# Second MLP, second stage: seven block products in place of eight, weights kept split in DRAM, first-stage sums gathered in PSUM

## The chip, the cores and the metric

One core of a Trainium2 chip runs the whole program. The time is device microseconds from launch to end, as the median of several executions; lower is better. TensorE is called PE, VectorE DVE, ScalarE ACT, GpSimd POOL and SyncE SP. SP issues every DMA of this program.

## The reference

Attention over chunks (4 batches, 8 heads, 768 positions, head size 64; each chunk of 32 positions sees itself, 16 positions before, 8 after and 8 memory positions) gives 3072 tokens of 512 values. Two MLPs follow, each with 512 x 2048 and 2048 x 512 weights:

```python
def _moe_ref(x, w_in, w_out):
    h = x @ w_in
    g = h * (1.0 / (1.0 + np.exp(-h)))
    return (g @ w_out).astype(np.float32)

def _moe2_ref(x, w_in, w_out):
    h = x @ w_in
    r = np.maximum(h, 0.0)
    g = r * r
    return (g @ w_out).astype(np.float32)
```

q, k, v and the memory keys and values are float32, the MLP weights float64 (the kernel reads them as 64-bit words); the output is float32.

## The kernel before

**Precision.** PE multiplies in a float32 form of reduced precision. So every operand is split in two: a high part (a rounding copy, mostly on ACT) and a low part (operand minus high part, on DVE or POOL), and each matrix product is three matmuls, high x low, low x high and high x high, added up in one PSUM bank. "A split" below is this pair of operations.

**Staging.** After attention for the first block, the first MLP works through six blocks of 512 tokens (`mlp`, line 688). A block has 16 steps, one for each 128 of the 2048 inner values: 12 matmuls into a `ph` bank, Silu and split, and, some two steps later, 12 matmuls into four `acc` banks. Attention of the next block lies between. The result goes to DRAM (`y1`), transposed. In the same time `convert_out` (line 589) turns the second MLP's output weights from 64-bit words to float32 and stores them to DRAM (`w2s`). In the last block `convert_forms` (line 610) prepares seven combinations of the input weights, split, which stay in SBUF.

**The second MLP.** It works through six blocks of 512 tokens, and each block through eight pairs: a pair is two of the sixteen 128-wide parts of d_ff, k and k + 8. Its first product (x times w_in) is done by the Strassen-Winograd scheme: the 2 x 2 blocked product of a pair takes seven block products in place of eight. `tokens` (line 794) makes the seven combinations of x and splits them; `stage_in` (line 860) does the products P1 to P7 in the order of `PRODUCTS`, each six matmuls of 256 columns into its own bank (four banks `ph`, `ph`, `sc`, `sc` in turn), and DVE adds them up to the four quarters of h (`plus`). Then h is squared after max(h, 0), split, and `stage_out` (line 960) multiplies it with w_out the plain way: for each of the pair's two parts four tiles of three matmuls of 512 columns, into four `acc` banks that gather over the whole block. `stage_in` also loads the two parts of w_out (256 KB each) and splits them, once in each block. `second` (line 982) lists the turns: products of pair k, then the second stage of pair k - 1. `evict` (line 745) copies the four `acc` banks out at a block's end and stores them.

**What sets the order.** Every operation is a piece with a cost on each engine that may do it, a due time, and the pieces that it needs. `Graph.order` (line 107) places the pieces by simulated time, in order of due time, and the program is issued in that order, so that each engine's queue and SP's queue of DMAs are fixed before the run. `on_tensor` (line 788) keeps the second MLP's products on PE in the order in which they are written. Operations that use the port that DVE and POOL share carry `port=True`, and the planner doesn't overlap them. Buffers are named by tag, with a count for each (`pool`), and a piece that takes a buffer waits for the last users of the one it replaces.

Of the kernel before, what the change touches and what calls it, by code (L numbers as in the profile page):

```python
# [59 lines left out]
PRODUCTS = (1, 6, 5, 7, 2, 3, 4)  # L60
# [123 lines left out]
def chunk_attention_two_mlps(ctx, tc, units, weights, out):  # L184
# [23 lines left out]
    w2s = dram.tile([FT, P, DM], F32, name="w2s")  # L208
# [45 lines left out]
    IN, OUT = 4.95, 5.56  # L254
    PAIR = IN + OUT
    BLOCK2 = PAIRS * PAIR
# [329 lines left out]
    def out_due(i):  # L586
        return step_due(1, 8) + i * 3.5 * BLOCK1 / FT

    def convert_out(i):

        due = out_due(i)
        wraw, got = load_words(i, 1, due)
        got.release = due - 25
        wu, d = words(1, i, 1, due, wraw, 0, got)

        def store(e):
            nc.sync.dma_start(out=w2s[i], in_=wu.tile)

        w2_kept[i] = G.add({"SP": 0.45}, due + 2, store, [d], uses=[wu], size=P * DM * 4)
# [88 lines left out]
    def mlp(j):  # L688
        accs, earlier = None, []
        size = step_due(j, 1) - step_due(j, 0)  # L690
        for i in range(FT):
# [34 lines left out]
            def back(e, i=i, wb=wb, g=g):  # L726
                w, t = wb.tile, g.tile
                first, last = i == 0, i == FT - 1
                for m, acc in enumerate(accs):
# [4 lines left out]
                    nc.tensor.matmul(o, w[:, 0, ws], t[:, 0], start=False, stop=last)  # L734

            y = G.add({"PE": 2.8}, due + 2.4 * size, back, [d, w_done[i, 1]],
# [4 lines left out]
        ends = evict(accs, [y], due, lambda m: y1[m, :, j * TB:(j + 1) * TB])  # L741
        stored[j] = ends
        return y

    def evict(accs, y, due, where, last=False):
        ends = []
        for m, acc in enumerate(accs):
            yb = G.buf("xq" if last and m == KT - 1 else "wr")

            if last and m == KT - 1:  # L750

                for n in range(2):
                    def part(e, n=n, acc=acc, yb=yb):
                        t = yb.tile if n else take(yb, [P, DM], F32, "y")
                        cs = slice(n * HALF2, (n + 1) * HALF2)
                        (nc.vector.tensor_copy if n else nc.scalar.copy)(t[:, cs], acc.tile[:, cs])  # L756

                    def store(e, n=n, m=m, yb=yb):
                        cs = slice(n * HALF2, (n + 1) * HALF2)
                        nc.sync.dma_start(out=where(m)[:, cs], in_=yb.tile[:, cs])  # L760

                    a = G.add({"DVE" if n else "ACT": 0.4}, due, part,
                              [y[m % len(y)]] + [yb.by] * n, new=[yb] * (not n),
                              uses=[acc] + [yb] * n)
                    G.add({"SP": 0.45}, due, store, [a], uses=[yb], size=P * HALF2 * 4)
                continue
# [27 lines left out]
    def tokens(b, due):  # L794
# [35 lines left out]
        xs, four = {}, []  # L830
        for rank, n in enumerate(X_FORM[p] for p in PRODUCTS):

# [17 lines left out]
            a = G.add({"ACT": 0.62}, due - 6 + 0.8 * rank, high,  # L850
                      [ready[n]] + ([] if new else [x.by]),
                      new=[x] * new, uses=[xf] + [x] * (not new))
            xs[n] = (x, at, G.add({"DVE": 0.72, "POOL": 1.35}, due - 5 + 0.8 * rank, low, [a],
# [3 lines left out]
    in_bank = itertools.cycle(("ph", "ph", "sc", "sc"))  # L857
    w_place = itertools.cycle((f"w{FT - 2}", f"w{FT - 1}"))

    def stage_in(k, xs, due):  # L860

        where, converted = forms[k]
        bank = {n: G.buf(next(in_bank)) for n in PRODUCTS}
        left, right = (0, HALF2), (HALF2, T2)
        one, two = G.buf("pr"), G.buf("pts")
        s1, u2, u4, u3 = (one, left), (one, right), (two, left), (two, right)
        h = [G.buf("xq") for _ in range(2)]
        made = {}

        def product(n):  # L870
            x, xa, x_done = xs[X_FORM[n]]
            fb, fa = where[W_FORM[n]]

            def emit(e):
                o = take(bank[n], [P, HALF2], F32, "pp")
                w, t = fb.tile[:, fa], x.tile[:, xa]
                for kt in range(2):
                    ws = slice(kt * P, (kt + 1) * P)
                    for at, (a, c) in enumerate(((1, 0), (0, 1), (0, 0))):
                        nc.tensor.matmul(  # L880
                            o, w[:, a, ws], t[:, c, kt],
                            start=(kt == 0 and at == 0), stop=(kt == 1 and at == 2),
                        )

            made[n] = on_tensor(0.71, due, emit, [x_done, *converted], [bank[n]], [fb, x])

        def plus(at, to, n, other, after):

            (tb, (t0, t1)), (ob, (o0, o1)) = to, other
            new = not tb.users  # L890

            def emit(e):
                if new:
                    take(tb, [P, T2], F32, "sums")
                nc.vector.tensor_tensor(  # L895
                    tb.tile[:, t0:t1], bank[n].tile, ob.tile[:, o0:o1], op=ALU.add
                )

            return G.add({"DVE": 0.45}, due + at, emit, [made[n], *after], new=[tb] * new,
                         uses=[bank[n]] + [ob] * (ob is not tb) + [tb] * (not new))  # L900

        def copy_p1(e):
            nc.scalar.copy(take(one, [P, T2], F32, "sums")[:, :HALF2], bank[1].tile)

        for n in PRODUCTS:
            product(n)
        a1 = G.add({"ACT": 0.4}, due + 1, copy_p1, [made[1]], new=[one], uses=[bank[1]])
        a2 = plus(1.2, u2, 6, s1, [a1])
        a4 = plus(1.4, u4, 5, u2, [a2])
        a3 = plus(1.6, u3, 7, u2, [a2, a4])  # L910
        c22 = plus(1.8, (h[1], right), 7, u4, [a4])
        c11 = plus(2.5, (h[0], left), 2, s1, [a1])
        c12 = plus(3.0, (h[0], right), 3, u4, [a4, c11])
        c21 = plus(3.5, (h[1], left), 4, u3, [a3, c22])
        done = []
        for n, after in enumerate(([c12], [c21])):
            g = G.buf("g")

            def square(e, n=n):
                t = h[n].tile  # L920
                nc.vector.scalar_tensor_tensor(t, t, 0.0, t, op0=ALU.max, op1=ALU.mult)  # L921

            def high(e, n=n, g=g):
                t = take(g, [P, 2, T2], F32R, "g2")
                nc.scalar.copy(t[:, 0], h[n].tile)  # L925

            def low(e, n=n, g=g):
                t = g.tile
                engine[e].tensor_tensor(t[:, 1], h[n].tile, f(t[:, 0]), op=ALU.subtract)  # L929

            d = G.add({"DVE": 0.75}, due + 4 + n, square, after, uses=[h[n]], port=True)
            d = G.add({"ACT": 0.62}, due + 5 + n, high, [d], new=[g], uses=[h[n]])
            done.append((g, G.add({"DVE": 0.75, "POOL": 1.35}, due + 6 + n, low, [d],
                                  uses=[h[n], g], port=True)))
        w2 = G.buf(next(w_place))
        split = []
        for n in range(2):
            wf = G.buf("wu")

            def load(e, n=n, wf=wf):  # L940
                nc.sync.dma_start(out=take(wf, [P, DM], F32, "wf"), in_=w2s[k + n * PAIRS])

            def high(e, n=n, wf=wf):
                if n == 0:
                    take(w2, [P, 2, 2, DM], F32R, "w2")
                nc.scalar.copy(w2.tile[:, n, 0], wf.tile)  # L946

            def low(e, n=n, wf=wf):
                t = w2.tile[:, n]
                engine[e].tensor_tensor(t[:, 1], wf.tile, f(t[:, 0]), op=ALU.subtract)  # L950

            d = G.add({"SP": 0.45}, due - 8 + n, load, [w2_kept[k + n * PAIRS]], new=[wf],
                      size=P * DM * 4)
            d = G.add({"ACT": 0.62}, due + 4 + n, high, [d, *([w2.by] if n else [])],
                      new=[w2] * (n == 0), uses=[wf] + [w2] * n)
            split.append(G.add({"DVE": 0.75, "POOL": 1.35}, due + 5 + n, low, [d],
                               uses=[wf, w2], port=True))
        return done, w2, split

    def stage_out(k, n, made, accs, due, final):  # L960
        done, w2, split = made
        g, ready = done[n]
        first, last = k == 0 and n == 0, k == PAIRS - 1 and n == 1
# [131 lines left out]
```

## Time and profile before

| | us |
|---|---|
| median of 3 runs | 1134.35 |
| lowest and highest | 1133.68, 1135.42 |
| profiled execution, span from first to last instruction | 1133.1 |

The profile is of one execution; no time other than its span is given for it. Busy time of an engine is the time that its instructions cover; matmuls overlap, so that the distance between the starts of two matmuls, and not the duration shown, is what one costs. The granted clock is that of PE as a share of 2.4 GHz. A wait is put down to what ended it.

### The profile page before, as it was taken

What the parts mean: (1) busy time and instruction counts of PE and PEld (TensorE: products, weight loads), DVE (VectorE), ACT (ScalarE), POOL (GpSimd) and SP (SyncE); (2) the same over time, 40 slices, a digit from 0 to 9 for tenths busy, and PEclk for the clock granted to TensorE, in tenths of its full rate; (3) what the DMA queues carried; (4) which work ended last, traced back from release to release, by engine and by line L of the source; (5) the groups of instructions that cost most, each with busy time, mean ns of one, the idle gap of its engine ahead of it and who ended that gap; (6) DMA issues with size and microseconds to landing.
All of it is one profiled execution on the core that took longest, in us unless ns stands there. A gap on an engine that the chain in (4) does not pass through costs nothing. (4 is left out here: it accounts for less than half of the span.)

```text
span 1133.1 us, 21204 instructions
## 1 busy us (share of the span) xinstructions
PE 1114.5 (98%) x8620; PEld 932.4 (82%) x8620; DVE 756.3 (67%) x1717; ACT 463.1 (41%) x781; POOL 120.9 (11%) x105
## 2 busy tenths in 40 slices
PE   6999999999999999999999999999999999999998
PEld 4777777777777777778888888988988988988987
DVE  4777668776677777665688656656656656656654
ACT  2788743443334444343576223323323323323321
POOL 0032200000000000000001211211211211211110
PEclk8899999999999999999999999999999999999999
DMA  7765334232234223222335213313313313211311
GB/s 276 262 215 187 104 113 141 75 122 75 94 112 149 78 76 122 76 90 75 105 118 161 64 38 93 94 38 93 94 38 94 93 38 94 93 38 57 93 38 37
DMA packets 52849, 114.81 MB, mean 101 GB/s; under 512 B 5520, under 2 KB 11920, under 8 KB 52752
## 3 DMA queue, kind: packets, MB, share of 16 engines
q1 hardware_dynamic: 52752, 113.46, 31.0%
q8 instruction: 67, 1.10, 0.4%
q14 instruction: 30, 0.25, 0.1%
HBM read 96.67 MB, written 16.78 MB: 100 GB/s over the span
## 5 line engine op out<-in xcount | busy, mean ns | idle before, releaser
L880 PEld LDWEIGHTS pp<-xs,forms 128*128 128x128 f32 x2016 | 247.2, 188 | 4.6 <-DVE sums L895 0.5
L880 PE MATMUL pp<-xs,forms 128*128 128x256 f32 x2016 | 248.6, 282 | 0.2 <-DVE sums L895 0.2
L895 DVE TENSOR_TENSOR sums<-pp,sums 128x256 f32<-128x256 f32 x336 | 135.9, 423 | 70.1 <-PE pp L880 66.2
L699 PE MATMUL ph<-x,w 128*128 128x512 f32 x384 | 156.3, 407 | 2.7 <-DVE w L568 2.0
L925 ACT CAST g<-sums 128x512 fp32r<-128x512 f32 x96 | 59.5, 620 | 230.1 <-DVE sums L921 188.0
L700 PE MATMUL ph<-x,w 128*128 128x512 f32 x384 | 153.5, 400 | 0.0
L701 PE MATMUL ph<-x,w 128*128 128x512 f32 x384 | 153.2, 399 | 0.0
L971 PE MATMUL acc<-w,g 128*128 128x512 f32 x384 | 152.4, 397 | 0.7 <-POOL g L929 0.7
L732 PE MATMUL acc<-g,w 128*128 128x512 f32 x384 | 152.5, 397 | 0.1
L733 PE MATMUL acc<-g,w 128*128 128x512 f32 x384 | 152.3, 397 | 0.0
L972 PE MATMUL acc<-w,g 128*128 128x512 f32 x384 | 151.9, 396 | 0.0
L734 PE MATMUL acc<-g,w 128*128 128x512 f32 x384 | 151.7, 395 | 0.0
L970 PE MATMUL acc<-w,g 128*128 128x512 f32 x384 | 151.7, 395 | 0.0
L707 ACT ACTIVATE ph<-ph 128x512 f32<-128x512 f32 x96 | 55.9, 582 | 223.6 <-PE ph L701 223.5
L950 POOL TENSOR_TENSOR w<-wf,w 128x512 fp32r<-128x512 f32 x47 | 60.9, 1295 | 411.6 <-ACT w L946 411.6
L714 DVE TENSOR_TENSOR g<-ph,g 128x512 fp32r<-128x512 f32 x96 | 66.1, 689 | 48.1 <-ACT g L711 46.8
L946 ACT CAST w<-wf 128x512 fp32r<-128x512 f32 x96 | 59.1, 622 | 92.7 <-PE acc L972 89.6
L387 DVE STREAM_TRANSPOSE turned<-pr 32x128 f32<-32x128 f32 x256 | 77.5, 303 | 25.4 <-ACT pr L398 20.7
L929 DVE TENSOR_TENSOR g<-sums,g 128x512 fp32r<-128x512 f32 x95 | 65.9, 697 | 39.4 <-ACT g L925 36.5
L699 PEld LDWEIGHTS ph<-x,w 128*128 128x128 f32 x384 | 72.7, 189 | 23.1 <-DVE w L568 2.8
L732 PEld LDWEIGHTS acc<-g,w 128*128 128x128 f32 x384 | 72.1, 188 | 18.6 <-DVE w L568 0.2
L701 PEld LDWEIGHTS ph<-x,w 128*128 128x128 f32 x384 | 72.9, 190 | 17.3
(73 smaller groups left out, 1356.9 us busy)
## 6 DMA issues: line engine op xcount, KB each, us to landing
wf<-w2s SPq DMA_DIRECT2D x96, 256.0 KB, 2.7
wraw<-weights SPq DMA_DIRECT2D x40, 512.0 KB, 4.4
raw<-units SPq DMA_DIRECT2D x48, 384.0 KB, 4.4
raw<-units SPq DMA_DIRECT2D x48, 260.0 KB, 4.9
w<-weights SPq DMA_DIRECT2D x24, 512.0 KB, 6.1
y<-y SPq DMA_DIRECT2D x24, 256.0 KB, 2.4
xf<-y SPq DMA_DIRECT2D x24, 256.0 KB, 4.0
out<-y SPq DMA_DIRECT2D x23, 256.0 KB, 2.1
```

The costliest lines, as they stand in the source:

```text
L387: nc.vector.transpose(out=t[rs, :, cs], in_=src.tile[cs, :, rs])
L699: nc.tensor.matmul(o, w[:, 1, ws], x[:, 0, kt], start=(kt == 0), stop=False)
L700: nc.tensor.matmul(o, w[:, 0, ws], x[:, 1, kt], start=False, stop=False)
L701: nc.tensor.matmul(o, w[:, 0, ws], x[:, 0, kt], start=False, stop=(kt == KT - 1))
L732: nc.tensor.matmul(o, w[:, 1, ws], t[:, 0], start=first, stop=False)
L733: nc.tensor.matmul(o, w[:, 0, ws], t[:, 1], start=False, stop=False)
L734: nc.tensor.matmul(o, w[:, 0, ws], t[:, 0], start=False, stop=last)
L880: nc.tensor.matmul(o, w[:, a, ws], t[:, c, kt], start=(kt == 0 and at == 0), stop=(kt == 1 and at == 2),)
L895: nc.vector.tensor_tensor(tb.tile[:, t0:t1], bank[n].tile, ob.tile[:, o0:o1], op=ALU.add)
L970: nc.tensor.matmul(o, t[:, 0, gs], w[:, 1], start=first, stop=False)
L971: nc.tensor.matmul(o, t[:, 1, gs], w[:, 0], start=False, stop=False)
L972: nc.tensor.matmul(o, t[:, 0, gs], w[:, 0], start=False, stop=last)
```

## The change

The second stage of the second MLP becomes a seven-product scheme too, in the Winograd form, over the pair's two parts of d_ff (inner), the two halves of the 512 tokens and the two halves of the 512 outputs. Each of the seven products is six matmuls of 256 columns. They gather over the eight pairs of a block in six banks or seven, and only at the block's end are they combined (`combine`, `finish`) into the four quarters of the output: one copy and six adds, and one more add for the product P4.

- **Weights.** `convert_out` now works on pairs: it forms the combinations of w_out that the scheme needs (four differences), splits all seven forms, and stores the split parts to DRAM: `w2s` is (pairs, 7 forms, 128, 2, 256). In the second MLP they are loaded as they are and no longer split there. Per pair, `load_pair` loads forms in DMAs of 512 KB (two forms) and 256 KB (one).
- **Second stage's left operand.** Per pair, four quarters of h squared, A11, A12, A21 and A22, and the sums S1 to S4 of them, are made on DVE and POOL (`sums`) and split two at a time (`split`). A22 is kept until the next block, where the fourth product uses it.
- **First stage.** Its products are no longer kept apart and added by DVE: P1, P6, P7 and P4 are matmuls into the same half bank one after the other, and ACT copies the running sum out between them (`visit`, `kept_sum`); P2 and P5 go to the halves of a second bank, P3 is added to P5's half. Three adds per pair stay on DVE.
- **Order.** One step has the pair n's seven first-stage products, three second-stage products of pair n - 1 and three of n - 2 in between; the fourth products of a block (eight) are done in the second and third pair of the next block, those of the last block at the end, into the two `sc` banks.
- **First MLP's end.** The last 12 matmuls of its last block are cut into four parts that lie between the first products of the second MLP.
- **Buffers.** `wr` has four instead of three.

The diff, cut to its core:

```diff
-PRODUCTS = (1, 6, 5, 7, 2, 3, 4)
+PRODUCTS = (1, 2, 5, 6, 7, 4, 3)
+BACK = (1, 5, 6, 7, 3, 2)
+NF = len(BACK) + 1
+BANK = {1: "acc", 5: "ph", 6: "acc", 7: "acc", 2: "acc", 3: "ph"}
...
-        ("wu", 4), ("wr", 3), ("nm", 3), ("sm", 4),
+        ("wu", 4), ("wr", 4), ("nm", 3), ("sm", 4),
...
-    w2s = dram.tile([FT, P, DM], F32, name="w2s")
+    w2s = dram.tile([PAIRS, NF, P, 2, HALF2], F32, name="w2s")
...
+        t1 = diff((0, 0), b(ua, 1), b(ua, 0), [da], True)
+        t2 = diff((0, 1), b(ub, 1), t(0, 0), [t1, db], False)
+        t3 = diff((1, 0), b(ub, 1), b(ua, 1), [da, db], True)
+        t4 = diff((1, 1), b(ub, 0), t(0, 1), [t2, t3], False)
...
+        split([0], ua, lambda: halves(ua.tile)[:, :1], [da], 2)
+        split([5, 4], ub, lambda: halves(ub.tile), [db], 3)
+        split([1, 2], z[0], lambda: z[0].tile, [t2], 4)
+        split([3, 6], z[1], lambda: z[1].tile, [t4], 5)
...
+    def front(q, x, due):
+        at = q.k % 2
+        q.kept = pairs[q.n - 1].kept if at else G.buf(next(saved))
+        a1 = visit(q, 0, ((1, 0),), x, due[0])
+        u1 = kept_sum(q, U1, 0, 0, [a1], due[0] + 0.9, new=True)
+        yield
+        b1 = visit(q, 1, ((2, 1), (5, 0)), x, due[1])
+        c11 = plus(q, (q.t, A11), 1, 1, U1, [u1, b1], due[1] + 5)
+        a11 = square((q.t, A11), [c11], due[1] + 11)
+        yield
+        a2 = visit(q, 0, ((6, 0),), x, due[2], [u1])
+        u2 = kept_sum(q, U2, 0, 0, [a2], due[2] + 0.9)
+        yield
+        a3 = visit(q, 0, ((7, 0),), x, due[3], [u2])
+        u3 = kept_sum(q, U3, 0, 0, [a3], due[3] + 0.9)
+        c22 = plus(q, (q.kept, at), 1, 0, U3, [u3, b1], due[3] + 1.4, new=not at)
+        a22 = q.a22 = square((q.kept, at), [c22], due[3] + 5)
+        yield
+        a4 = visit(q, 0, ((4, 0),), x, due[4], [u3])
+        c21 = kept_sum(q, A12, 0, 0, [a4], due[4] + 0.9, func=AF.Relu)
+        a12 = square((q.t, A12), [c21], due[4] + 9)
+        yield
+        b2 = visit(q, 1, ((3, 0),), x, due[5], [c22, c11])
+        c12 = plus(q, (q.t, A21), 1, 0, U2, [b2], due[5] + 1)
+        a21 = square((q.t, A21), [c12], due[5] + 2.4)
+        s1 = sums(q, S1, (q.t, A21), (q.kept, at), ALU.add, [a21, a22], due[5] + 3)
+        s3 = sums(q, S3, (q.t, A11), (q.t, A21), ALU.subtract, [a21, a11], due[5] + 4.5)
+        s2 = sums(q, S2, (q.t, S1), (q.t, A11), ALU.subtract, [s1, a11], due[5] + 5)
+        s4 = sums(q, S4, (q.t, A12), (q.t, S2), ALU.subtract, [a12, s2, s1, s3], due[5] + 8)
...
+    def multiply(o, g, at, w, wat, first, last, alone=None):
+        for m in range(2):
...
+            for r, (a, c) in enumerate(((0, 1), (1, 0), (0, 0))):
+                nc.tensor.matmul(
+                    out_, g[:, at, a, gs], w[:, wat, c],
...
+    def load_pair(q, due, past=()):
+        load_some(q, 0, 2, "wraw", due - 10)
+        for k in range(4 if past else 0):
+            load_fourth(past[k:k + 1], "wu", due - 11 + k)
+        for j in (2, 3):
+            load_some(q, j, 1, "wu", due - 9 + j + (2 if past else 0))
+        if past:
+            for k in range(4, PAIRS):
+                load_fourth(past[k:k + 1], "wu", due - 8 + k)
+        load_some(q, 4, 2, "wraw", due - 5)
...
+            slots = [
+                [], [(two, 3)], [(two, 4), (two, 5)], [(one, 0), (one, 1)], [], [(one, 2)],
+            ]
+            if q.k == 1 and past:
+                slots[2] += past[:2]
+                slots[3] += past[2:3]
+                slots[4] += past[3:4]
+                slots[5] += [(one, 3)]
+            if q.k == 2 and past:
+                slots[0] = past[4:6]
+                slots[1] = past[6:]
```

In `front`, each `yield` ends one of the six slots of a step, and the products listed in `slots` follow it on PE. `one` and `two` are the pairs before the present one.

## Rows read from the trace of the kernel before

**Rows 1.** The page: busy time of each engine; granted clock in 40 slices.

```profile
PE 1114.5 (98%) x8620; PEld 932.4 (82%) x8620; DVE 756.3 (67%) x1717; ACT 463.1 (41%) x781; POOL 120.9 (11%) x105
...
PEclk8899999999999999999999999999999999999999
```

**Rows 2.** Busy us by stretch: length; PE, PEld, DVE, ACT, POOL; clock; DMA share; GB/s.

```profile
0.00:34.00 34.00, 22.17 (x564) 14.97 (x565) 19.18 (x52) 10.89 (x18) 2.69 (x12) 0.82 0.80 286
...
228.00:326.00 98.00, 98.00 (x900) 77.46 (x899) 70.02 (x201) 39.98 (x60) 0.00 (x0) 1.00 0.31 103
...
721.00:805.00 84.00, 84.00 (x522) 75.23 (x521) 53.67 (x105) 25.80 (x48) 15.32 (x12) 1.00 0.25 76
```

**Rows 3.** PE's waits in the whole span: us in total, times, longest.

```profile
PE po L413 <- issue: 4.8, 2, 2.8
...
PE acc L971 <- POOL g L929: 0.7, 1, 0.7
...
PE pp L880 <- DVE sums L895: 0.2, 1, 0.2
```

**Rows 4.** The chain of waits in order of time: start, us, what.

```profile
701.58 4.99 PE pp L880 x42
...
786.58 4.99 PE pp L880 x42
...
1129.15 0.25 PE acc L972
...
1129.48 0.38 ACT y L756
...
1129.88 0.42 DVE y L756
```

**Rows 5.** Timeline of one pair, PE: start, us, engine, line, operation, tiles, count.

```profile
741.07 5.18 PE L880 MATMUL pp<-xs,forms 128*128 128x256 f32 x42
...
746.09 0.39 PE L970 MATMUL acc<-w,g 128*128 128x512 f32 x1
...
751.47 0.40 PE L972 MATMUL acc<-w,g 128*128 128x512 f32 x1
...
751.70 1.47 PE L880 MATMUL pp<-xs,forms 128*128 128x256 f32 x11
```

**Rows 6.** Timeline of the same pair, ACT and DVE; idle time before in brackets.

```profile
742.03 0.37 ACT L903 COPY sums<-pp 128x256 f32<-128x256 f32 x1
...
742.30 0.62 ACT L946 CAST w<-wf 128x512 fp32r<-128x512 f32 x1
...
743.41 0.42 DVE L895 TENSOR_TENSOR sums<-pp,sums 128x256 f32<-128x256 f32 x1 [0.22 <-PE pp L880]
...
746.63 1.28 DVE L921 SCALAR_TENSOR_TENSOR sums<-sums 128x512 f32<-128x512 f32 x2
```

**Rows 7.** Timeline at the second MLP's start, POOL and PE.

```profile
628.02 1.27 POOL L929 TENSOR_TENSOR g<-sums,g 128x512 fp32r<-128x512 f32 x1 [1.86 <-ACT g L925]
...
629.34 0.50 PE L971 MATMUL acc<-w,g 128*128 128x512 f32 x1 [0.73 <-POOL g L929]
```

**Rows 8.** Groups by line: busy us, mean ns of one, idle before.

```profile
L624 DVE TENSOR_TENSOR wr<-wu 128x256 f32<-128x256 f32 x13 | 5.1, 421 | 0.0
...
L714 DVE TENSOR_TENSOR g<-ph,g 128x512 fp32r<-128x512 f32 x96 | 66.1, 689 | 48.1 <-ACT g L711 46.8
...
L950 POOL TENSOR_TENSOR w<-wf,w 128x512 fp32r<-128x512 f32 x47 | 60.9, 1295 | 411.6 <-ACT w L946 411.6
```

**Rows 9.** DMA issues: KB each, median us from issue to landing.

```profile
wf<-w2s SPq DMA_DIRECT2D x96, 256.0 KB, 2.7
...
wraw<-weights SPq DMA_DIRECT2D x40, 512.0 KB, 4.4
```

**Rows 10.** Timeline at a block's edge, POOL and DVE.

```profile
713.88 1.31 POOL L820 TENSOR_TENSOR xf<-xf 128x512 f32<-128x512 f32 x1
...
714.88 1.46 DVE L921 SCALAR_TENSOR_TENSOR sums<-sums 128x512 f32<-128x512 f32 x2
```

More of the change, by code (lines that the diff above doesn't have):

```diff
@@ L584, in chunk_attention_two_mlps, with out_due @@
     w2_kept = {}
[L586 to L599, printed above, removed]
+    def out_due(k):
+        return step_due(1, 8) + k * 3.5 * BLOCK1 / PAIRS
@@ L740, in mlp, with store, part, evict @@
         due = step_due(j, FT) + 2.0 * size
[L741 to L745, printed above, removed]
+        def store(ys):
+            stored[j] = evict(accs, ys, due, lambda m: y1[m, :, j * TB:(j + 1) * TB])
+        if j < NB - 1:
+            store([y])
+            return y, []
+        ys = []
+        def part(at, m):
+            ys.append(on_tensor(MM, at, lambda e: back(e, some=[m]), [d, w_done[FT - 1, 1]], [],
+                                [wb, g, accs[m]]))
+            if m == KT - 1:
+                store(ys)
+        return y, [lambda at, m=m: part(at, m) for m in range(KT)]
+    def evict(accs, y, due, where):
         ends = []
         for m, acc in enumerate(accs):
[L748 to L766, printed above, removed]
+            yb = G.buf("wr")
             def copy(e, acc=acc, yb=yb):
@@ L830, in tokens @@
         xs, four = {}, []
+        need = [1.5 * rank for rank in range(7)]
         for rank, n in enumerate(X_FORM[p] for p in PRODUCTS):
@@ L887, in plus @@
-        def plus(at, to, n, other, after):
-            (tb, (t0, t1)), (ob, (o0, o1)) = to, other
-            new = not tb.users
-            def emit(e):
[L893 to L957, printed above, removed]
@@ new lines, in emit, with kept_sum @@
+                            start=first and kt == 0 and r == 0, stop=kt == 1 and r == 2,
+                            skip_group_check=True,
+                        )
+        ready = [xs[X_FORM[n]][2] for n, _ in products]
+        return on_tensor(
+            MM * len(products), due, emit, [*ready, *converted, *after], [b] * first,
+            [where[W_FORM[n]][0] for n, _ in products] + [xs[X_FORM[n]][0] for n, _ in products]
+            + [b] * (not first),
+        )
+    def kept_sum(q, to, bank, h, after, due, func=AF.Copy, new=False):
+        def emit(e):
+            t = take(q.t, [P, 6, HALF2], F32, "sums") if new else q.t.tile
+            nc.scalar.activation(t[:, to], q.bank[bank].tile[:, h], func)
+        return G.add({"ACT": 0.4}, due, emit, after, new=[q.t] * new,
+                     uses=[q.bank[bank]] + [q.t] * (not new))
@@ new lines, in plus, with emit, square @@
+    def plus(q, to, bank, h, other, after, due, new=False):
+        def emit(e):
+            t = take(to[0], [P, 2, HALF2], F32, "kept") if new else to[0].tile
+            nc.vector.tensor_tensor(
+                t[:, to[1]], q.bank[bank].tile[:, h], q.t.tile[:, other], op=ALU.add
+            )
+        return G.add({"DVE": 0.45}, due, emit, after, new=[to[0]] * new,
+                     uses=[q.bank[bank], q.t] + [to[0]] * (not new))
+    def square(where, after, due):
+        def emit(e):
+            t = where[0].tile[:, where[1]]
+            nc.vector.scalar_tensor_tensor(t, t, 0.0, t, op0=ALU.max, op1=ALU.mult)
+        return G.add({"DVE": 0.45}, due, emit, after, uses=[where[0]], port=True)
@@ new lines, in sums, with emit, split, read @@
+    def sums(q, to, a, b, op, after, due):
+        def emit(e):
+            engine[e].tensor_tensor(
+                q.t.tile[:, to], a[0].tile[:, a[1]], b[0].tile[:, b[1]], op=op
+            )
+        return G.add({"DVE": 0.45, "POOL": 0.78}, due, emit, after, uses=[q.t, a[0], b[0]],
+                     port=True)
+    def split(src, first, after, due):
+        g = G.buf("g")
+        def read():
+            return src.tile[:, first:first + 2]
+        def high(e):
+            nc.scalar.copy(take(g, [P, 2, 2, HALF2], F32R, "g2")[:, :, 0], read())
+        def low(e):
+            t = g.tile
+            engine[e].tensor_tensor(t[:, :, 1], read(), f(t[:, :, 0]), op=ALU.subtract)
+        a = G.add({"ACT": 0.63}, due, high, after, new=[g], uses=[src])
+        return g, G.add({"DVE": 0.72, "POOL": 1.35}, due + 0.7, low, [a], uses=[src, g],
+                        port=True)
@@ new lines, in chunk_attention_two_mlps, with split_kept, fourth, emit @@
+    kept_split = {}
+    def split_kept(b, n, due):
+        q, r = (pairs[b * PAIRS + 2 * n + i] for i in range(2))
+        kept_split[b, n] = split(q.kept, 0, [q.a22, r.a22], due)
+    def fourth(q, due, last_block):
+        b, k = q.b, q.k
+        (g, ready), (w, wat, loaded) = kept_split[b, k // 2], q.fourth
+        first, last = k == 0, k == PAIRS - 1
+        if first:
+            banks[b, 4] = [G.buf("sc") for _ in range(2)] if last_block else [G.buf("acc")]
+        bank = banks[b, 4]
+        def emit(e):
+            for m, one in enumerate(bank):
+                o = take(one, [P, 2, HALF2], F32, "out") if first else one.tile
+                multiply(o, g.tile, k % 2, w.tile, wat, first, last, m if last_block else None)
+        p = on_tensor(MM, due, emit, [ready, loaded], bank if first else [],
+                      [g, w] + ([] if first else bank))
+        if last:
+            banks[b, 4, "done"] = p
@@ new lines, in finish, with emit @@
+    def finish(b, u3, after, due):
+        bank = banks[b, 4]
+        for m, one in enumerate(bank):
+            def emit(e, m=m, one=one):
+                if len(bank) == 1:
+                    nc.vector.tensor_tensor(u3.tile, one.tile, u3.tile, op=ALU.add)
+                else:
+                    t = u3.tile[:, m]
+                    nc.vector.tensor_tensor(t, one.tile[:, 0], t, op=ALU.add)
+            d = G.add({"DVE": 0.72 / len(bank)}, due, emit, [banks[b, 4, "done"], *after],
+                      uses=[one, u3])
+            store(b, u3, 1, 0, d, due, None if len(bank) == 1 else m)
```

289 lines of the change are left out of this document (217 added, 72 removed).

## The prediction

> **What bounds the kernel now.** I read the page first: PE is busy for 98% of the span, every other engine far less, and the granted clock stands at its upper level (2.4 GHz) in all slices but the first few [rows 1]. The busy times by stretch say the same stage by stage: in a block of the first MLP and in a block of the second, PE is busy for the whole stretch at clock 1.00, while DVE has 28 us of 98 and 30 us of 84 free, and ACT more [rows 2]. The list of waits leaves nothing to win from waiting: PE's whole wait in the second MLP is 0.7 and 0.2 us, both in its first two pairs [rows 3]. The chain of waits is one run of matmuls to 1129.40, then two half evictions and the last store [rows 4]. So only the number and the spacing of matmuls sets the time; anything else matters only where it makes PE wait.
>
> **The terms, from the traced pair.** One pair (two of the 16 blocks of d_ff, one block of 512 tokens) starts its 42 products matmuls of 256 columns at 741.07, its 24 matmuls of 512 columns at 746.09, and the next pair starts at 751.70 [rows 5]. So 42 take 5.02 us, 0.1195 each; 24 take 5.61 us, 0.2338 each; a pair is 10.63 us. The chain's marks give the same over a whole block: 786.58 - 701.58 = 85.00 us for 8 pairs [rows 4].
>
> **Removed and added on PE.** Per pair the 24 matmuls of 512 columns go, and seven products of six 256-column matmuls come, 42 more. The new ones differ from the stage-one products only in which operand is the stationary one, so I give them the same 0.1195: a pair becomes 84 x 0.1195 = 10.04 us, 0.59 less. Bounds for one new matmul: below, half of the 512 one, 0.117 (a pair 9.93); above, the spacing at which nothing is won, 5.61 / 42 = 0.1336. I take 0.1195, because it is measured on the same shape. 48 pairs: -28.3 us. The fourth product of each pair is held back and done one block later, eight in a row of turns; this moves matmuls and adds none. The last piece of the first MLP's work is cut in four and laid between the first pair's products: same matmuls, no time.
>
> **Hand-offs of a bank.** Before, seven products went round four PSUM banks; now one bank takes P1, P6, P7, P4 in turn, and ACT must copy the running sum out before the next product may add to it. PE fills the gap with products of the two pairs before: two between P6 and P7, two between P7 and P4, one after P3 (one product is 5.02 / 7 = 0.717 us). So ACT has 1.43 us where the gap is two. What it needs: from a product's last issue slot to ACT's or DVE's start about 0.25 us (the first product's slot ends at 741.07 + 0.717 = 741.79, the copy starts at 742.03), 0.37 for the copy [rows 5, 6], and back to PE 0.05 (POOL ends 629.29, PE starts 629.34) [rows 7]: 0.67 us. With one split of 0.62 ahead of it on ACT [rows 6] it is 1.29, still inside. The other edges: c22 must be added after the copy of U3 and before P3 is accumulated, 0.67 + 0.42 = 1.1 of 2.15 us; c12 after P3 and before the next pair's second product, 0.25 + 0.42 + 0.05 = 0.72 of 1.43 us, or 1.41 with one 0.69 operation ahead of it. These waits are new; behind a waiting product all of PE's queue waits. Bound: nothing, or, with two operations ahead at every one of four edges, about 0.5 us each, 2 us a pair. I take nothing for steady pairs, nearer to the rows, since one operation ahead is what a 0.7 us queue entry means and the order puts the urgent one first. In the first two pairs there are few older products to fill with: 1 us in all.
>
> **DVE, ACT and POOL in the second MLP.** Per pair DVE now has three adds from PSUM and four squares and four sums, of 0.42 us each at 256 columns, and 3.5 splits of 0.69 [rows 8]: 11 x 0.42 + 2.4 = 7.0 us. It loses seven adds, two squares and four splits, 2.95 + 1.4 + 2.8 = 7.1. So the load hardly moves, while the pair is 0.59 shorter; POOL takes a few at 1.3 us [rows 8] as now. ACT has four copies and 3.5 splits, 3.7 us of 10.04. What is late next is the block's edge: seven splits of the new tokens, four of the kept product, six adds and one more for the result (0.69 each) come within two pairs, 18 x 0.69 = 12.4 us beside 2 x 7.0, in about 22 us of PE time: full, but the products that need them come spread over the same 22 us. I take 0.7 us of PE wait at each of five edges, bounds 0 and 3.
>
> **DMA and SP.** Each pair now loads 7 x 256 KB instead of 2 x 256 KB. A block moves 56 x 0.262 + 8 x 0.262 = 16.8 MB in 80 us, 209 GB/s; the kernel's first 34 us moved 286 GB/s with the engines 80% busy [rows 2], so the rate is there. A 512 KB load lands in 4.4 us, a 256 KB one in 2.7 [rows 9]; the 512 KB buffers come free about 7.9 us ahead of their next use, so nothing waits. SP takes its instructions in order, and a load waiting for its buffer holds what is behind it: worst where eight held-back products use four buffers; by my count of slots their loads have 0.7 to 1.4 us to spare. This is in the 0.7 per edge.
>
> **The first MLP.** The new weight forms are made there: per pair of rows four sums (0.42) and four splits (0.42 + 3 x 0.69) more, 4.2 us of DVE, eight times 33 us, spread over 3.5 blocks, some 340 us; ACT gets about 18, SP 56 stores instead of 16. DVE goes from 70 to about 80 us of 98 [rows 2]. The cover is its free 28 us; and PE does a step's second half some two steps after its first, so that the chain of ACT and DVE between them (0.6 + 0.6 + 0.7 us) has several us to spare. I take nothing. If the cover failed altogether it would cost the 33 us. The first 130 us have one more buffer for words: -1 to +1.
>
> **The end.** Two adds of 0.42 (now a copy of 0.38 and one of 0.42) [rows 4, 6], then 128 KB stores as now: 0.
>
> **Sum.** -28.3 for the products, -0.9 for the two waits that go with the old first pairs [rows 3], +1 start, +3.5 edges, +1 for small waits in the steady pairs: -23.7. Profiled span 1133.1, so 1109.4; the median of the runs, 1134.35, lies 1.25 above the span, and I keep that: 1110.6 us. With no new wait at all it is 1105.
>
> **A rule weighed.** Two squares on DVE that began while POOL still had 0.31 us to run took 1.46 us together against 1.28 where POOL was idle [rows 10, 6]: DVE was held. The Trainium skill's page "SBUF — State Buffer", section "SBUF: two separate sides", says why: the port pair of VectorE and GpSimd is an exclusive lock for the whole instruction, taken by a VectorE operation with two SBUF inputs and by GpSimd. The trace agrees. By the row the loss is 0.2 us; by the rule it may be a whole POOL instruction, and the change has more such DVE operations per pair.
>
> **Rivals.**
> (a) My forecast, 1105 to 1118. Chance 0.64.
> (b) The hand-offs cost a little in each pair: ACT or DVE is one operation late at one of four edges, 0.25 us a pair, +12 us: about 1122 (1118 to 1130). For: gaps of 1.43 us with 1.3 to 1.4 needed when one operation is ahead. Against: seven-product rounds with DVE adds on 2.15 us of slack never made PE wait. Chance 0.18.
> (c) Weights late at block edges: 3 us at each of five, +11 over my sum, 1122. For: four buffers for ten loads. Against: 286 GB/s. Chance 0.05.
> (d) Slower. A square or sum on DVE is caught by a POOL split of 1.29 us, and c22 or c12, which reads PSUM and needs no such port, stands behind it in DVE's queue; its chain is then 0.72 + 1.29 = 2.01 us, 0.6 past the 1.43 us that PE gives it, and with one more operation of 0.69 ahead PE waits 1.3 us. Once a pair that is 48 x 1.3 = 62 us: 1173; it decides from 0.5 us a pair, where the 24 us are eaten. This is the mechanism of the rule above. For: 11 of 14.5 DVE operations a pair are short and tightly tied. Against: POOL is busy 15 us of a block of 84 already [rows 2] and PE never waited for it after the start. Chance 0.09.
> (e) The change does not do what it says: the new products run at 0.133 a matmul because operands change more often; then 1134. Against: the products' own spacing. Chance 0.04.
>
> **How the numbers follow.** Faster by over 0.2% (2.3 us, about what a measurement here can tell from no change) holds in (a), (b), (c): 0.87. Same: (e), 0.04. Slower: (d), 0.09. The range is 1104 to 1126: all of (a), (c) and most of (b); what is left out is the upper end of (b), (d) and (e).
>
> **What would show it.** In the changed trace: products of the second stage at 0.119 to 0.120 each and pairs every 10.04 us in the middle of a block; blocks of 80.5 to 82 us; PE waits in the second MLP of 3 to 9 us in total, most within two pairs of a block's first; DVE near 80 of 98 us in the first MLP's blocks 1 to 4 with PE still whole. It is wrong if PE waits for ACT copies or DVE adds in every pair, if it waits for loads of the split weights, or if PE waits for DVE or ACT in the first MLP's blocks 1 to 4.

## The result, and the profile after

The changed kernel takes 1118.13 us (median of 4 runs, 1113.99 to 1119.26) against 1134.46 us. The ratio of the runs is 0.9846, with a 95% interval of 0.9825 to 0.9868 (the two medians alone give 0.9856). It is 16.3 us faster; the forecast was 23.8 us faster, 1110.6 us, within 1104 to 1126. The profiled execution took 1117.68 us with a span of 1115.8 us.

The page of the kernel after, busy time by engine and DMA share in 40 slices (tenths):

```profile
PE 1089.7 (98%) x9484; PEld 957.5 (86%) x9484; DVE 806.9 (72%) x1818; ACT 517.3 (46%) x926; POOL 182.0 (16%) x171
...
DMA  7875344343334432431343556756756766755756
```

PE is still busy 98% of the span, with 24.8 us less than in [rows 1]. The DMA engines, which the page's queue line has busy for 31% of the span before, have 52% now, and the digits show that the second MLP (the right half) has most of it. Busy time by stretch of the kernel after (columns as in [rows 2]): a block of the first MLP, then a block of the second:

```profile
228.00:326.00 98.00, 98.00 (x900) 77.45 (x899) 73.50 (x204) 42.96 (x66) 11.03 (x11) 1.00 0.40 136
...
781.00:862.00 81.00, 79.19 (x664) 78.82 (x663) 59.96 (x116) 33.00 (x68) 18.80 (x16) 1.00 0.67 204
```

In the first MLP PE is whole, as before. In this block of the second it lacks 1.8 us, which it did not in [rows 2]. The waits of PE in the second MLP of the kernel after, with its first and last pairs (us in total, times, longest):

```profile
PE out L1071 <- DMA w<-w2s: 10.4, 8, 2.7
PE out L1071 <- POOL g L1004: 0.9, 2, 0.5
PE pp L942 <- ACT sums L959: 0.5, 1, 0.5
```

Of 11.8 us, 10.4 are waits for the split weights. The timeline shows where they are not: two marks of neighbouring steady pairs on PE.

```profile
645.26 1.59 PE L942 MATMUL pp<-xs,forms 128*128 128x256 f32 x12
...
654.54 1.59 PE L942 MATMUL pp<-xs,forms 128*128 128x256 f32 x12
```

A step without held-back products is 13 products, 78 matmuls, in 9.28 us: 0.119 us each, and no wait between them. The waits stand at the blocks' edges. Here are three lines of the first edge: SP issuing the loads, the load that PE waited for (from the chain of waits), and PE after the wait. Below them stand the stretches around the edge:

```profile
702.54 14.03 SPq L1016 DMA_DIRECT2D w<-w2s  x9
...
703.25 6.95 DMA w<-w2s
...
710.25 2.93 PE L1071 MATMUL out<-w,g 128*128 128x256 f32 x12 [2.74 <-DMA w<-w2s]
```

```profile
690.00:700.00 10.00, 10.00 (x87) 10.00 (x86) 8.50 (x18) 4.32 (x9) 3.59 (x4) 1.00 0.78 263
700.00:710.00 10.00, 7.50 (x64) 7.30 (x62) 9.16 (x14) 3.64 (x7) 6.26 (x5) 1.00 0.97 339
710.00:720.00 10.00, 9.75 (x70) 9.76 (x71) 4.36 (x10) 2.64 (x5) 0.73 (x1) 0.83 0.46 139
...
740.00:770.00 30.00, 30.00 (x255) 30.00 (x254) 21.82 (x46) 13.29 (x29) 3.52 (x4) 1.00 0.59 174
```

Look at the last three columns. In mid-block the DMA engines are 59% busy at 174 GB/s; in the ten us of the edge they are 97% busy at 339 GB/s, a load of 256 KB lands 7 us after its issue, and PE is idle a quarter of the time. After the wait of 2.74 us twelve matmuls take 2.9 us instead of 1.6. The granted clock of the next stretch is 0.83 on average, so for a part of it the clock was at its lower level (1.2 GHz).

### The profile page after: what moved, and what is told of

It is laid out like the page before. It is cut to its first block, busy times and chain, and to the rows that moved or that the text cites. A ratio compares the mean times of both kernels' runs of the same rounds, so it can differ in the third digit from the quotient of the medians.

```text
span 1115.8 us, 23506 instructions
## 1 busy us (share of the span) xinstructions
PE 1089.7 (98%) x9484; PEld 957.5 (86%) x9484; DVE 806.9 (72%) x1818; ACT 517.3 (46%) x926; POOL 182.0 (16%) x171
## 4 chain that ended last, share of the span: by engine, by line
PE 92%; DMA 5%; issue 1%; SPq 1%; POOL 0%; DVE 0%; ACT 0%; POOLq 0%
PE pp L942 20%; PE out L1071 20%; PE ph L756 9%; PE ph L758 8%; PE acc L790 8%; PE ph L757 8%; PE acc L792 8%; PE acc L791 8%; DMA w<-w2s 3%; PE po L417 2%; PE sc L331 2%; DMA xf<-y 1%; PE turned L382 1%; DMA raw<-units 1%; DMA w<-weights 1%
## 5 line engine op out<-in xcount | busy, mean ns | idle before, releaser
L1071 PE MATMUL out<-w,g 128*128 128x256 f32 x2016 | 275.6, 284 | 11.5 <-DMA w<-w2s 10.4
L942 PE MATMUL pp<-xs,forms 128*128 128x256 f32 x2016 | 272.3, 281 | 0.5 <-ACT sums L959 0.5
L1071 PEld LDWEIGHTS out<-w,g 128*128 128x128 f32 x2016 | 255.7, 192 | 13.6 <-DMA w<-w2s 9.0
L942 PEld LDWEIGHTS pp<-xs,forms 128*128 128x128 f32 x2016 | 253.7, 189 | 1.6 <-ACT sums L959 1.1
L1004 DVE TENSOR_TENSOR g<-sums,g 128x512 fp32r<-128x512 f32 x132 | 104.3, 790 | 65.4 <-ACT g L1000 65.4
L959 ACT ACTIVATE sums<-pp 128x256 f32<-128x256 f32 x192 | 74.0, 386 | 159.1 <-PE pp L942 127.6
L1000 ACT CAST g<-sums 128x512 fp32r<-128x512 f32 x144 | 89.3, 620 | 120.0 <-PE out L1071 116.3
L978 DVE SCALAR_TENSOR_TENSOR sums<-sums 128x256 f32<-128x256 f32 x144 | 65.8, 466 | 35.2 <-ACT sums L959 33.0
L792 PEld LDWEIGHTS acc<-g,w 128*128 128x128 f32 x384 | 72.1, 188 | 17.7
L790 PEld LDWEIGHTS acc<-g,w 128*128 128x128 f32 x384 | 72.1, 188 | 17.2 <-DVE w L572 0.2
L791 PEld LDWEIGHTS acc<-g,w 128*128 128x128 f32 x384 | 72.1, 188 | 17.1
```

The source lines that it names most:

```text
L942: nc.tensor.matmul(o[:, at], w[:, a, ws], t[:, c, kt], start=first and kt == 0 and r == 0, stop=kt == 1 and r == 2, skip_group_check=True,)
L959: nc.scalar.activation(t[:, to], q.bank[bank].tile[:, h], func)
L1000: nc.scalar.copy(take(g, [P, 2, 2, HALF2], F32R, "g2")[:, :, 0], read())
L1004: engine[e].tensor_tensor(t[:, :, 1], read(), f(t[:, :, 0]), op=ALU.subtract)
L1071: nc.tensor.matmul(out_, g[:, at, a, gs], w[:, wat, c], start=first and r == 0 and (m == 0 or alone is not None), stop=last and r == 2, sk ...
```

## The experiments

The first MLP ends at a different time in each run: the second MLP's first product starts between 612.3 and 616.4 us in the profiles of all these kernels. So beside the time each run has **the length of the second MLP**, from its first to its last matmul in the profile, which that does not touch: 499.1 us in the changed kernel, with 9.0 us of waits for weights at the five edges and 1.4 at the end.

Three theories stood against each other. A: the edge fills the DMA queue. B: four small buffers for ten loads, so that each load is issued only when PE frees one. C: SP takes its instructions in order, and stores that wait for DVE hold up the loads behind them.

**Tokens later.**

```diff
             p = G.add({"SP": 0.45}, due - 50 + n, load, after, ...)
             p.behind += loads[:1]
+            if b:
+                p.release = due - 50 + n
```

> Edit: the four loads of the next block's tokens (1 MB) may not start earlier than 50 us before that block; in the changed kernel they start as soon as their buffer is free, right at the block's edge. Theory A (at each edge the DMA queue is full: tokens, stores of the result and held-back weights come within 15 us and land late): each burst ends about 2.9 us earlier (4 x 0.72), PE's waits for split weights fall from 10.4 us to 3 to 4 (the last 1.9 at the end stay), time from 1118 to 1109 to 1112. Rival B (the four small buffers: a load can be issued only when PE has freed one, whatever else the queue carries): waits and time unchanged, 1117 to 1119. Rival C (SP stands behind stores that wait for DVE): unchanged too.

Measured 1121.4 us (1120.8 to 1124.7), ratio 0.9881 (0.9863 to 0.9900); second MLP 504.4 us. Waits of PE in the second MLP, and the first edge's stretch:

```profile
PE out L1073 <- DMA w<-w2s: 11.2, 9, 2.9
PE pp L944 <- DVE kept L970: 3.2, 3, 1.4
PE pp L944 <- DVE sums L970: 1.0, 2, 0.5
```

```profile
702.00:712.00 10.00, 7.80 (x66) 7.59 (x64) 8.46 (x16) 3.64 (x7) 2.60 (x2) 1.00 0.98 323
```

All of A's numbers failed here: the tokens leave the edge, and the edge is as full (0.98) and as late as before. And new waits for DVE come in mid-block; with them the time is also above the 1117 to 1119 of B and C. In the changed kernel the four token loads are issued by 693.8 us and land within 5.3 us, so they had landed before the crowd; what crowds is something else.

**Stores later.**

```diff
-        G.add({"SP": 0.45}, due, emit, [after], uses=[y],
+        p = G.add({"SP": 0.45}, due, emit, [after], uses=[y],
               size=P * HALF2 * 4 * (2 if m is None else 1))
+        if b < NB2 - 1:
+            p.release = due + 20
```

> Edit: the three result stores of each block but the last are held back by some 20 us, out of the edge; tokens load as in the changed kernel. Theory A (full queue): 3 to 4 us less in each burst, waits for split weights down to 3 to 5 us, 1110 to 1113. Rival B (buffers): 1117 to 1119. Rival C (SP behind stores that wait for DVE): the edges' waits vanish altogether, 1108 to 1110, while the tokens' move alone gives nothing.

(The late fourth store of a block is held back too.) Measured 1109.0 us (1107.1 to 1110.1), ratio 0.9764 (0.9748 to 0.9781); second MLP 491.1 us.

```profile
PE out L1071 <- DMA w<-w2s: 4.2, 5, 1.3
```

```profile
700.00:710.00 10.00, 9.03 (x76) 8.82 (x75) 9.15 (x13) 3.64 (x7) 6.60 (x5) 1.00 0.84 262
```

The edge is 84% full, the waits fall by 6.2 us, and the granted clock stays at 1.00. B as it was put (the buffers alone, whatever else the queue carries) falls, because the buffers are the same and the waits are not. The waits lie in A's range and the time in C's, so A and C are still to be parted. One half of B holds all the same. In the changed kernel SP waits for PE to free a buffer before most of these loads:

```profile
SPq L1016 <- PE out L1071: 350.2, 217, 5.8
```

So most of the 240 loads could not have been issued earlier, and the landing time then decides whether a load comes late. More buffers, which would let the loads start earlier, were not tried.

**Thin stores** part these two: the same stores at the same place in SP's order, with one eighth of the bytes.

```diff
                 to = out[r0:r0 + HALF2, cs].rearrange("(m p) c -> p m c", m=2)
-                nc.sync.dma_start(out=to, in_=y.tile)
+                n = 16 if b < NB2 - 1 else P
+                nc.sync.dma_start(out=to[:n], in_=y.tile[:n])
```

> Edit: in all blocks but the last, each result store takes 16 of the 128 partitions; seven eighths of the output are left out. The same instructions in the same order on SP, with the same waits for DVE. Theory A (the bytes of the stores in the queue): as with the stores moved away, waits 4 to 5 us, 1108 to 1111. Rival C (SP stands at a store until DVE has made its data, and the loads behind it are issued late): waits and time unchanged, 1117 to 1119.

Measured 1112.7 us (1108.5 to 1115.1), ratio 0.9808 (0.9782 to 0.9835); second MLP 491.5 us, the same as with the stores moved away.

```profile
PE out L1071 <- DMA w<-w2s: 4.7, 7, 1.2
```

```profile
703.40:713.40 10.00, 9.23 (x78) 9.02 (x77) 9.16 (x15) 3.73 (x8) 6.49 (x5) 1.00 0.85 276
```

The second MLP of this profile began 3.4 us later than in the changed kernel (at 616.2 us), so the stretch of its first edge does too. Without these 3.4 us the profiled execution's 1113.5 us would lie in the range that A gave. The waits are where A put them. The 256 KB load that PE waits for at the first edge tells the same. Counted from the second MLP's first product it is issued at 90.5 us in the changed kernel, 91.1 with the stores later and 91.0 with thin stores, so never earlier; but it lands 6.95, 5.2 and 5.0 us after its issue. C falls: what the stores carry counts, not SP's place in line. A thin store has fewer bytes and fewer packets; the next run takes packets alone away.

**Whole rows.** The half rows that the change writes are 1 KB runs, and before it 2 KB. This run writes 2 KB runs again, at wrong rows.

```diff
+                    nc.sync.dma_start(
+                        out=out[at:at + P, :], in_=y.tile.rearrange("p m c -> p (m c)")
+                    )
```

> Edit: in all blocks but the last, each result store writes whole rows of 2 KB (128 rows) in place of half rows of 1 KB (256 rows): the same bytes at the same place in the order, but at wrong rows of the output. Theory A1 (the short runs are what makes a store hold the queue 1.3 us, where 256 KB of weights land 0.66 us apart): PE's waits for split weights fall from 10.4 to about 7 us, 1113 to 1115. Theory A2 (a store holds it for being a store, whatever its runs): waits and time as in the changed kernel, 1117 to 1119.

Measured 1119.4 us (1114.8 to 1121.2), ratio 0.9865 (0.9838 to 0.9892); second MLP 500.7 us.

```profile
PE out L1071 <- DMA w<-w2s: 9.4, 8, 1.9
```

Its waits for POOL are longer (1.8 us against 0.9), so that PE waits for the two together as long as in the changed kernel, 11.2 against 11.3 us. Only the wait at the first edge is shorter, 1.9 against 2.7 us. The length of the runs is not what costs the time (A1 falls), and so it is the bytes.

**One load**, the bound:

```diff
+        if tag in once:
+            return once[tag]
         w = G.buf(tag)
...
+        once[tag] = w, G.add({"SP": 0.45}, due, emit, after, new=[w], ...)
+        return once[tag]
```

> Leaves out nearly all loads of the second MLP's split output weights: each buffer kind is loaded once and every pair multiplies with it, so that PE's products are the same in number and order. All theories in which loads cost the time (A, B, C): no wait for split weights, about 14 us less than the changed kernel (waits 10.4, slow matmuls after the longest 1.4, re-starts 2): 1103 to 1105. If bank hand-offs, DVE or the shared port were hidden behind these waits, part comes back as waits for ACT, DVE or POOL: 1108 or more.

Measured 1103.4 us (1101.4 to 1104.7), ratio 0.9713 (0.9693 to 0.9732); second MLP 483.9 us. PE's only wait there:

```profile
PE pp L942 <- ACT sums L959: 0.5, 1, 0.5
```

So the loads of split weights are the whole of it: 15 of the 499 us (13 by the repeat of the changed kernel, below). Nothing of bank hand-offs, DVE or POOL was hidden behind them.

**All moves, then two of them.** In the last block the held-back weights can be loaded early, into buffers of first-stage weights that this block no longer needs:

```diff
-        for k in range(half):
-            load_fourth(past[k:k + 1], "wu", t - 8 + MM * k)
+        for k in range(2):
+            load_fourth(past[half * k:half * (k + 1)], f"w{2 + k}", t - 40 + 2 * k)
         load_pair(one, t + 7 * MM)
-        for k in range(half, PAIRS):
-            load_fourth(past[k:k + 1], "wu", t + MM * k)
```

With tokens and stores both later:

> Edit: both moves, and in the last block the eight held-back weights come in two loads of 1 MB into two buffers of first-stage weights that this block has done with, some 40 us ahead of use. Theory A: edges below 1 us of wait in all, the end's 1.9 us gone: 1104 to 1108. Rival B: the end's 1.9 us alone, 1115 to 1117. Rival C: as A.

Measured 1111.9 us (1108.3 to 1114.8), ratio 0.9786 (0.9764 to 0.9808); second MLP 493.5 us. That misses A's 1104 to 1108. The second MLP is 2.4 us longer than with the stores' move alone, but in time the two can't be told apart (0.9786 and 0.9764, with overlapping intervals). With the tokens left as in the change:

> Edit: stores held back by some 20 us, and the last block's eight held-back weights in two early loads of 1 MB; tokens as in the changed kernel. Expected if tokens loaded at the edge cost little and the end is short of loads alone: waits for split weights 3 to 4 us, none at the end, 1106.5 to 1108.5, one us under the stores' move alone (1109.0). If the tokens' move was worth something in the run that had all three: no better than that one, 1110 to 1112.

Measured 1106.8 us (1106.3 to 1110.4), ratio 0.9770 (0.9748 to 0.9793); second MLP 486.9 us.

```profile
PE out L1071 <- DMA w<-w2s: 1.1, 3, 0.6
PE pp L942 <- ACT sums L959: 0.5, 1, 0.5
PE out L1071 <- POOL g L1004: 0.4, 1, 0.4
PE pp L942 <- DVE kept L968: 0.3, 1, 0.3
```

This version beats both kernels, and comes within 3 us of the second MLP without loads. Over the stores' move alone its gain is not shown: the ratios are 0.9770 and 0.9764. Up to the fifth edge SP issues the same DMAs in the same order in both, and still the waits at the edges are 1.1 us in this profile and 3.7 in the other. So the waits of one profile are good to some 3 us, and of the two versions' 4.2 us in the second MLP only the wait at the end (0.5 us, none here) can be put down to the early loads. The edges of the changed kernel stand clear of this: 9.0 us, and 8.9 in its repeat.

**What the tokens' move cost.** The timeline of the version with all moves, in mid-block, where POOL makes token sums:

```profile
819.43 5.59 POOL L877 TENSOR_TENSOR xf<-xf 128x512 f32<-128x512 f32 x4 [7.07 <-DMA xf<-y]
...
822.36 2.94 DVE L987 TENSOR_TENSOR sums<-sums 128x256 f32<-128x256 f32 x2
...
826.34 0.97 PE L944 MATMUL pp<-xs,forms 128*128 128x256 f32 x6 [2.00 <-ACT sums L961]
```

Two DVE sums that take 0.75 us elsewhere in this trace take 2.94 while POOL works; ACT's next split waits for them, the copy of a running sum stands behind that split, and PE waits 2.00 us. This is rival (d) in another form: POOL's token sums in place of its splits, and ACT's queue in place of DVE's. To test it, the token sums were put on DVE alone, with the tokens' move alone:

```diff
-            return G.add({"DVE": 0.72, "POOL": 1.35}, at, emit, after, uses=[xf], port=True)
+            return G.add({"DVE": 0.72}, at, emit, after, uses=[xf], port=True)
```

> Edit: the tokens' loads held back as in the first experiment, and the four sums of tokens of each block on DVE alone instead of DVE or POOL. Theory P (in the first experiment POOL's token sums, 1.3 us each, held DVE's short operations on two SBUF operands in the steady pairs, and ACT's and PE's queues behind them): PE's waits for DVE and ACT sums in mid-block go from 4.2 to 1 us or less, DVE's squares and sums there are back at 0.42 us, waits for weights at the edges stay at 10 to 12 us; 1116 to 1119 against 1121.4. Rival (the tokens' bytes in mid-block, or DVE's load): the waits stay at 3 to 5 us, 1120 to 1122.

Measured 1122.4 us (1121.8 to 1125.0), ratio 0.9903 (0.9887 to 0.9920): no gain in time. The second MLP is 501.1 us against 504.4, and in mid-block 2.4 us of waits stay of 4.2. PE's waits, and DVE at one such place:

```profile
PE out L1073 <- DMA w<-w2s: 10.8, 8, 2.6
PE pp L944 <- DVE kept L970: 2.4, 3, 0.9
```

```profile
822.82 0.69 DVE L877 TENSOR_TENSOR xf<-xf 128x512 f32<-128x512 f32 x1 [2.54 <-DMA xf<-y]
```

DVE's sums there are back at 0.42 us, as theory P had it, and PE still waits. So the hold by POOL is a part at most. The other part is DVE standing at the first token sum for 2.54 us until its load lands, with the urgent sums behind it: two waits of 0.90 us recur in both runs (at 910.25 and 992.80 us with the tokens later, 906.88 and 989.79 here), each behind a DVE wait of 1.7 to 2.3 us for a token load. Putting the token sums on DVE did not change these 1.8 of the 4.2 us; how the rest is shared is open.

**How much margin a hand-off has.** On the version with two moves, ACT makes each copy of a running sum two or three times:

```diff
-            nc.scalar.activation(t[:, to], q.bank[bank].tile[:, h], func)
+            for _ in range(2):
+                nc.scalar.activation(t[:, to], q.bank[bank].tile[:, h], func)
```

> On the version with the stores held back and the early loads for the end (it has 1.1 us of waits for weights, so that others can be seen): ACT makes each of the four running-sum copies of a pair twice, 0.39 us more; the order of all work stays. The prediction had the hand-off need 0.67 us of the 1.43 that PE gives it. Theory H (that margin is real): 0.67 + 0.39 = 1.06, still inside: no wait for ACT in steady pairs, time within 2 us of 1106.8. Rival (the margin is nearly used up already, by what stands ahead on ACT and DVE): 0.2 us or more a pair, 10 us or more in all.

> The same with each copy made three times: 0.67 + 2 x 0.39 = 1.45 us against 1.43. Theory H: the margin is just gone: small waits for ACT in each pair, and with one split of 0.62 ahead of a copy 0.6 us; 10 to 40 us slower than 1106.8. If the time still does not move, the need was mis-stated by half a microsecond; if it is more than 50 us slower, work queued behind the copies counts for more than the copies.

Twice: 1109.4 us in its one run. That is 2.7 us over the version it is made from, more than the 2 us that H allowed, but within that version's own runs (1106.3 to 1110.4). The second MLP takes 489.2 against 486.9 us; the difference lies in the first pairs, which lack fill, and at the edges, and there are no waits in steady pairs. Three times: 1132.3 us in its one run, 26 us over. Two marks of neighbouring pairs of the latter on PE:

```profile
649.92 1.70 PE L942 MATMUL pp<-xs,forms 128*128 128x256 f32 x12
...
659.72 1.70 PE L942 MATMUL pp<-xs,forms 128*128 128x256 f32 x12
```

A step takes 9.80 us against 9.28: PE waits a little, about 0.1 us, at four places a pair. In steady pairs the second copy is free and the third is not, as the sum of 0.67 + 0.39 a copy against 1.43 us said. The sum left the third only 0.02 us short at each place and the run has 0.13; three copies take 1.22 us in this trace, where the sum had 1.17.

**The changed kernel again**, beside the second set of runs:

> No edit: the changed kernel once more on this chip, as the measure for the runs beside it. Expected 1114 to 1119, waits for split weights 9 to 11 us at the same places.

Measured 1119.5 us (1116.5 to 1120.0), just above the range given, ratio 0.9867 (0.9845 to 0.9888); second MLP 497.3 us, waits for weights 10.5 us.

## Why the prediction was right, and where its size was off

- **The product count: right.** 84 matmuls of 256 columns a pair, at 0.119 instead of 0.1195 us. Over 4032 matmuls the difference is 2 us to the good. Without loads the second MLP takes 483.9 us, 481.1 after the last 2.8 us of the first MLP that lie in it; the prediction had 4032 x 0.1195 = 481.8 before any wait.
- **Hand-offs of a bank: right.** Nothing in steady pairs, and 0.5 us where the first pairs have no older products to fill with. That one wait measures the round trip: between the starts of the last P6 matmul and of P7 lie 0.76 us in the trace, 0.64 without the matmul's own slot, where 0.67 was worked out. The two runs with more copies show that the margin was as large as said. Rival (b) falls.
- **DVE, ACT, POOL and the first MLP: right in effect.** PE has no wait in the first MLP's blocks 1 to 5. DVE rose by 3.5 us a block instead of 10 ([rows 2]), because POOL took 11 us.
- **DMA and SP: the step that failed.** It set a block's mean, 209 GB/s, against 286 GB/s seen at the start, and took the rate to be there; the landing times of a quiet queue (2.7 and 4.4 us, [rows 9]) then gave 0.7 to 1.4 us to spare. But the loads are not even: within about 15 us of an edge come eight held-back weights, three stores and a pair's own weights. At the first edge the queue runs at 97% and 339 GB/s, and loads land up to 7 us after issue. The mean itself was right (204 GB/s in the block shown). The term was 0.7 us per edge, 3.5 in all. It measured 9.0 us of waits in the five edges, and 13.4 us when the 0.9 us of waits for POOL, the slow matmuls after the longest wait and the short re-starts are counted (1.7 to 4.4 an edge). So PE's waits in the second MLP are 11.8 us where the prediction looked for 3 to 9, blocks two to five take 81.6 to 84.4 us where it looked for 80.5 to 82, and one of its own signs of being wrong came true: PE waits for loads of the split weights. Rival (c) had the effect and its price, 3 us an edge, and was given 0.05; its reason, four buffers for ten loads, is the half that keeps the loads from starting earlier. The edges' stores are the part that tips it: with them moved away or thinned the second MLP is 6 to 8 us shorter.
- **The end: off by 1.9 us.** It was costed at nothing by looking at the last adds alone. Before them come eighteen second-stage products in a row (108 matmuls in the trace). Each multiplies with 256 KB of weights and takes 0.71 us, so that this stretch needs weights twice as fast as a mixed one.
- **Rival (d)** did not cost time in the changed kernel: PE's 0.9 us of waits for POOL are for splits that POOL itself made. But what it rests on happens there too, at the first edge, where POOL's three token sums (701.70 to 706.34) stretch a square on DVE from 0.41 to 1.52 us (the line below) and PE has no wait for it. It reached PE when the tokens' sums were moved among steady pairs. The rule of the page "SBUF — State Buffer" of the Trainium skill, section "SBUF: two separate sides", that the port pair is locked for the whole instruction, fits the 2.94 us above; the 0.2 us that was read from [rows 10] was a lower end. Each of those two sums was held for about 1.1 us, less than one of POOL's operations (5.59 us for four).

```profile
702.23 1.52 DVE L978 SCALAR_TENSOR_TENSOR sums<-sums 128x256 f32<-128x256 f32 x1
```

- **The sum** for the profiled execution: 1109.4 forecast, 1115.8 measured. +9.9 at the edges, +1.9 at the end, -1 for the small waits of steady pairs that did not come, -2 for the matmuls' spacing, -2.1 because this run's first MLP ended early: 6.7, of 6.4. The time lies 1.9 us above the span, where 1.25 was carried over. The early end of the first MLP is luck (between profiles of the same kernel the second MLP began at 612.8 and 616.4 us), and with the two other gains it hides 5 of the 12 us by which the edges and the end were underrated.

## What to carry to other kernels

A mean rate over a block says nothing of a burst: count the bytes due within one landing time of each crowded place, stores among them, set those against the highest rate that the trace shows, and ask how early the buffers let a load start. Stores are free to wait, loads in front of a waiting engine are not; with one queue, hold the stores back by a release time, and leave early transfers early. What reuses a bank needs its whole round trip (drain, copy, semaphore) covered by other work, and that can be summed from the trace to a tenth of a microsecond.

## What the runs showed of the hardware that was not expected

- PE's granted clock fell to its lower level after some waits in the second MLP, and for some 14 to 17 matmuls they were 0.21 us apart, 1.2 to 1.6 us on top of the wait. It fell after 2.7 us in the changed kernel, 2.9 with the tokens later, 2.6 with the token sums on DVE, 2.0 with all moves, and 1.9 and 1.8 with whole rows. It did not fall after 2.7 us in the repeat of the changed kernel, nor after any wait of 1.7 us or less. So the wait's length alone does not settle it; what does was not tried.
- One queue moved 339 GB/s in a stretch of 10 us at 97% busy, more than the 286 GB/s that the start had shown. At that rate a 256 KB load landed 6.95 us after its issue, where the median of such loads in the whole run is 3.2. Over all loads and stores of the split weights (256 and 512 KB) the trace has:

```profile
DMA to landing us min/median/max: 2.0/3.6/7.0
```
